# A fused attention and two-layer network kernel: the first 512 tokens by pairs of heads, parts of g and x out of PSUM, and rooms on the right 128 bytes further

## The chip, the cores and the metric

The kernel runs on one core of a Trainium2 chip. The metric is the device time of one execution in microseconds; the median of several runs is compared.

## The reference, cut to what matters

```python
def attention(q, k, v, g_norm):                  # [8 batches, 8 heads, 576, 64]
    kv = np.einsum('bhsd,bhse->bhde', k, v)      # one 64x64 matrix for each head
    out = np.einsum('bhsd,bhde->bhse', q, kv)
    rms = np.sqrt(np.mean(out * out, axis=-1, keepdims=True) + 1e-06)
    return out / rms * g_norm

x = attention(...).transpose(0, 2, 1, 3).reshape(4608, 512)   # tokens x heads*64
h = x @ w_in                       # 512 -> 2048
x = (h * np.cos(h)) @ w_out        # 2048 -> 512
h = x @ w_in2                      # 512 -> 1024
# softmax-weighted h, layer norm over 1024, then @ w_out2: 1024 -> 512
```

All inputs are float32, and some weights are rebuilt on the core from pairs of words.

## The kernel before, in words

Every large product is done as three float32r matmuls: high times high, high times low and low times high (`mm3`, lines 171 to 173). So each operand has to be split into a high part (a copy rounded to float32r) and a low part (operand minus high part).

The tokens are taken in nine blocks of 512 (`NB`, `TB`). The kernel has three stages. In the first (to about 305 us) attention is computed, and with it the *first quarter* of the first network: 4 of its 16 chunks of 128 hidden columns. A *step* is one block of tokens times one such chunk: `step_h` computes h = x @ w_in for it, in a PSUM bank, as 4 chunks of x (128 of the 512 features each) with 3 matmuls each; `cosine` makes g = h cos(h) and its two parts in six operations (a rounding on ScalarE, a subtraction on VectorE, a sine on ScalarE, the product on VectorE, the high part on ScalarE, the low part on VectorE); `step_out` multiplies g with w_out into four other banks. Steps alternate between banks 0 and 1. In the second stage (305 to 900 us) the other three quarters follow, by a scheme with seven products (`first_h`, `first_out`), in the third the second network (`second`, `soft`, `second_out`).

Attention goes by batches and tiles. `kv_slots` loads K and V of a batch's four pairs of heads, multiplies them (line 495), and copies the 64x64 results into the block-diagonal tile `kvf` (line 513). `tile_slots` takes a tile of 128 tokens: four q products into one bank (line 552), the square on ScalarE (560), the sum over each head on VectorE (562), a power on GpSimd (569 and 570), the norm on VectorE (584), four transposes back into the same bank (589), a scaled copy to `xf` on ScalarE (593), and for every second tile a store of `xf` to DRAM (597), which the second stage reads again. `pair_prep` then splits `xf` into the high and low part of x (lines 394 and 395). `convert` rebuilds a weight chunk (lines 366 to 377: a copy on ScalarE and five VectorE operations, the last of them on GpSimd for later weights), and `split` makes its parts.

All operations are handed to a planner (`Flow`), with a duration, a due time `at` and keys that they read and write. It works through them by its own durations: whenever an engine is free it takes the ready operation with the earliest `at`. That fixes the order on each engine's queue, SP's queue of DMAs included; on the chip each queue is worked off in that order, each instruction waiting for its inputs. `W_LOAD` holds the due times of the first eight weight loads. Operations on VectorE and GpSimd that both use SBUF exclude each other in the planner; those marked `ps=True` don't.

SBUF rooms are allocated from the left or from the right end. On the right lie `edge` (unused, 32 bytes a partition), then the attention pools, later `rxb`, `mid` and `rg2`. `rxa`, `rg`, `rwo` and the others lie on the left. The two attention banks after the first six uses are banks 6 and 7 in turn (`late_att`).

Of the kernel before, what the change touches and what calls it, by code (L numbers as in the profile page):

```python
# [17 lines left out]
P = 128  # L18
# [34 lines left out]
CV_AHEAD, W_LOAD = 15, (-40, -14, 0, 6, 10, 14, 18, 22)  # L53
# [106 lines left out]
def tile_kernel(ctx, tc, qkv, tail, g2, w1, w2, gl, out):  # L160
# [36 lines left out]
    declare("edge", "edge", 0, [P, 8])  # L197
# [154 lines left out]
    def convert(src, sk, yk, wk, at, load_at, on_dve, wide=1.3):  # L352
# [15 lines left out]
        add("DVE", 0.43, lambda: DVE.tensor_scalar(out=a(), in0=a(), scalar1=3, scalar2=None,  # L368
                                                   op0=ALU.logical_shift_left), r=[yk], w=[yk], at=at)
        add("DVE", 0.71, lambda: DVE.scalar_tensor_tensor(out=a(), in0=word(1), scalar=0x80000000, in1=a(),  # L370
                                                         op0=ALU.bitwise_and, op1=ALU.bitwise_or),
            r=[yk, sk, ("half", sk)], w=[yk], at=at)
        add("DVE", 0.43, lambda: DVE.tensor_scalar(out=buf[wk].bitcast(U32), in0=a(), scalar1=0xFF800000, scalar2=None,
# [107 lines left out]
    Q_CUTS = (0, 2 * P, S)  # L481

    def kv_slots(b):
        n, bks = ("kvf", b % 2), [att_bank() for _ in range(2)]

        def pair(bk, p, w, at):
            j = b * NPAIR + p
            kv, tl = kv_key("kv", j), kv_key("tl", j)

            def mm():  # L490
                for c in range(5):
                    for e in range(2):
                        k_, v_ = (buf[tl], P) if c == 4 else (buf[kv], 512)
                        at_ = e * D if c == 4 else c * P + e * D
                        PE.matmul(buf[bk][e * D:(e + 1) * D, p % 2 * D:(p % 2 + 1) * D], lhsT=k_[:, at_:at_ + D],  # L495
                                  rhs=k_[:, v_ + at_:v_ + at_ + D], start=(c == 0), stop=(c == 4))

            kv_load(j, at - (ATT_LEAD if b else 0))
            if b == 0:
                q_load(j, at + 3, Q_CUTS)  # L500
            add("PE", KV_T, mm, r=[kv, tl] + ([bk] if p % 2 else []), w=w + ([] if p % 2 else [bk]), at=at)

        def slot(half):
            def run(at):
                bk = bks[half]
                done = [("kvp", b, p) for p in range(2 * half, 2 * half + 2)]
                for i, d in enumerate(done):
                    pair(bk, 2 * half + i, [d], at)
# [24 lines left out]

    def tile_slots(g):
        bks = [att_bank() for _ in range(2)]

        def heads(ap):
            return ap.rearrange("p (n w) -> p n w", w=D)

        def first(h, at):  # L540
            t, i, bk, sq = 2 * g + h, (2 * g + h) % 4, bks[h], stage()
            for b, a, n, row in parts(t):
# [12 lines left out]
                for p in range(NPAIR):  # L555
                    add("PE", 0.222, lambda p=p, mm=mm: mm(p=p),
                        r=[kvf, *(("kvfh", kvf, i, e) for i in range(2) for e in range(2)), qs[p],
# [7 lines left out]
        def rms(h, at):  # L565
            i = (2 * g + h) % 4

            def power():
                POOL.tensor_scalar(out=buf["ss", i], in0=buf["ss", i], scalar1=1e-6, scalar2=None, op0=ALU.add)
                POOL.tensor_tensor(out=buf["y", i], in0=buf["ss", i], in1=buf["mhalf"], op=ALU.pow)  # L570

            add("POOL", POW, power, r=["mhalf"], w=[("ss", i), ("y", i)], at=at, ps=True)

        def second_(h, at):
# [18 lines left out]
            add("ACT", 0.61, lambda: ACT.activation(out=buf[xf][:, :, h * P:(h + 1) * P], in_=tr(), func=AF.Copy,  # L593
# [6 lines left out]
        def slot(h):  # L600
            def run(at):
# [3 lines left out]
                if h and g < NU - 2:  # L605
                    pair_prep(g, at - XPRI)
# [6 lines left out]
    def prep(src, keys, dst, hk, lk, at, lo_dve):  # L613
# [12 lines left out]
        def op(out_, fn, in0, in1, r, w):  # L626
            add("POOL", 0.75, lambda: POOL.tensor_tensor(out=out_(), in0=in0(), in1=in1(), op=fn), r=[*keys, *r], w=w, at=at)  # L627
# [15 lines left out]


# [3 lines left out]
    for i, name in enumerate(("xo0", "xo1", "rg2x")):  # L648
        for n in ("xhk", "xlk"):
            for j in range(4):  # L650
                flow.pool_of[n, i, j // 2, j % 2] = name

# [9 lines left out]
    def cosine(h, psrc, tk, n, hi, lo, r, hk, lk, t, on_dve):  # L662

        def tt():
# [9 lines left out]
        add("DVE", e_(0.71, 0.44, n), lambda: DVE.tensor_tensor(out=tt(), in0=h(), in1=tt(), op=ALU.mult),  # L674
            r=[*r, tk], w=[tk], at=t, ps=psrc)
# [538 lines left out]
```

## Time and profile before

| | us |
|---|---|
| median of 3 runs | 1290.01 (1287.57 to 1291.79) |
| profiled execution | 1292.3 |
| its span, first to last instruction | 1290.4 |
| TensorE busy | 1257.6 |
| VectorE / ScalarE / GpSimd busy | 930.3 / 677.9 / 518.3 |

The profile has a page of the whole execution and views of its trace: busy time by stage, groups of instructions by line, the waits and what released them, and the timeline. PE is TensorE, DVE is VectorE, ACT is ScalarE, POOL is GpSimd, SP the queue that issues the DMAs. Times are microseconds, or nanoseconds where it says so.

### The profile page before, as it was taken

How to read it: one execution, taken by the hardware profiler on the slowest of the kernel's cores; microseconds unless marked ns; L12 is line 12 of the kernel's file. 1: busy time of each engine (PE TensorE's matmuls, PEld its weight loads, DVE VectorE, ACT ScalarE, POOL GpSimd, SP SyncE). 2: the span in 40 equal slices, each digit the busy share in tenths (PEclk: the TensorE clock that was granted, in tenths of full speed). 3: DMA queues.
4: the chain of work that ended last, by engine and by line, in shares of the span. 5: the costliest groups of instructions: out<-in, count | busy, mean ns of one | idle time of the engine just before them, and what ended most of it. 6: DMA issues, size and time to landing. Idle time of an engine off the chain costs nothing.

```text
span 1290.4 us, 18723 instructions
## 1 busy us (share of the span) xinstructions
PE 1257.6 (97%) x6576; PEld 1066.5 (83%) x6576; DVE 930.3 (72%) x1544; ACT 677.9 (53%) x1225; POOL 518.3 (40%) x510
## 2 busy tenths in 40 slices
PE   5899999999999999999999999999999999999998
PEld 4688888887999899888788888887888888888887
DVE  6777777777887687878787766565777677776753
ACT  4666766675663563645364534442555545454533
POOL 2246656756745666554543443221321212121000
PEclk8899999999999999999999999999999999999999
DMA  8888899568948858663774374387111111111000
GB/s 278 292 264 283 286 326 304 191 216 282 336 152 227 285 184 276 211 227 115 241 221 157 101 212 136 107 284 237 59 56 50 50 42 56 43 50 42 25 25 33
DMA packets 177406, 224.59 MB, mean 174 GB/s; under 512 B 10912, under 2 KB 115360, under 8 KB 177312
## 3 DMA queue, kind: packets, MB, share of 16 engines
q1 hardware_dynamic: 177312, 223.39, 53.4%
q8 instruction: 52, 0.85, 0.3%
q14 instruction: 42, 0.34, 0.1%
HBM read 156.77 MB, written 66.58 MB: 173 GB/s over the span
## 4 chain that ended last, share of the span: by engine, by line
PE 75%; POOL 3%; DVE 3%; DMA 2%; issue 2%; ACT 1%; SPq 0%; POOLq 0%; ACTq 0%; DVEq 0%
PE ps L171 24%; PE ps L172 24%; PE ps L173 24%; PE ps L932 2%; POOL rg L677 1%; PE ps L552 1%; POOL fconv L419 1%; POOL fconv L377 1%; POOL ws L395 1%; DMA px<-fh 1%; PE ps L589 1%; DMA xf<-xd 0%; DMA bd<-ws 0%; PE ps L495 0%; DMA wid<-ws 0%
## 5 line engine op out<-in xcount | busy, mean ns | idle before, releaser
L171 PE MATMUL ps<-rg,rwo 128*128 128x512 f32 (+1 forms) x912 | 349.5, 383 | 1.6 <-ACT rg L676 1.6
L172 PE MATMUL ps<-rg,rwo 128*128 128x512 f32 (+1 forms) x912 | 346.6, 380 | 1.2 <-POOL rg L677 1.2
L173 PE MATMUL ps<-rg,rwo 128*128 128x512 f32 (+1 forms) x912 | 346.4, 380 | 0.0
L677 POOL TENSOR_TENSOR rg<-fh,rg 128x512 fp32r<-128x512 f32 (+1 forms) x120 | 149.3, 1253 | 174.4 <-ACT rg L676 161.5
L171 PEld LDWEIGHTS ps<-rg,rwo 128*128 128x128 f32 x912 | 171.9, 188 | 30.7 <-ACT rg L676 1.9
L172 PEld LDWEIGHTS ps<-rg,rwo 128*128 128x128 f32 x912 | 171.7, 188 | 30.3 <-POOL rg L677 2.2
L173 PEld LDWEIGHTS ps<-rg,rwo 128*128 128x128 f32 x912 | 171.6, 188 | 29.4
L914 POOL TENSOR_TENSOR const<-const,const 128x1 f32<-128x1 f32 x36 | 20.9, 580 | 333.2 <-DVE const L901 300.0
L171 PE MATMUL ps<-rxa,rwi 128*128 128x512 f32 (+1 forms) x384 | 147.3, 383 | 1.4 <-DVE fh L862 0.8
L172 PE MATMUL ps<-rxa,rwi 128*128 128x512 f32 (+1 forms) x384 | 145.6, 379 | 1.2 <-DVE rxa L395 1.2
L173 PE MATMUL ps<-rxa,rwi 128*128 128x512 f32 (+1 forms) x384 | 145.2, 378 | 0.0
L667 ACT ACTIVATE fh<-ps 128x512 int32<-128x512 f32 (+1 forms) x126 | 71.3, 567 | 103.4 <-PE ps L173 83.3
L672 ACT ACTIVATE fh<-fh,const 128x512 f32<-128x512 f32 (+1 forms) x156 | 106.6, 690 | 32.6 <-DVE fh L669 31.7
L171 PE MATMUL ps<-rxb,rwi 128*128 128x512 f32 (+1 forms) x288 | 112.7, 391 | 4.8 <-DVE fh L757 3.0
L676 ACT CAST rg<-fh 128x512 fp32r<-128x512 f32 (+1 forms) x156 | 90.6, 586 | 41.6 <-DVE fh L674 39.5
L173 PE MATMUL ps<-rxb,rwi 128*128 128x512 f32 (+1 forms) x288 | 110.4, 383 | 0.0
L172 PE MATMUL ps<-rxb,rwi 128*128 128x512 f32 (+1 forms) x288 | 109.9, 381 | 0.0
L669 DVE SCALAR_TENSOR_TENSOR fh<-ps,fh 128x512 f32<-128x512 f32 (+1 forms) x126 | 81.2, 648 | 28.3 <-ACT fh L667 25.6
L674 DVE TENSOR_TENSOR fh<-ps,fh 128x512 f32<-128x512 f32 (+1 forms) x126 | 80.9, 647 | 24.8 <-ACT fh L672 24.5
L627 POOL TENSOR_TENSOR sf<-xf 128x256 f32<-128x256 f32 x72 | 62.6, 876 | 61.9 <-DMA xf<-xd 32.5
L171 PEld LDWEIGHTS ps<-rxa,rwi 128*128 128x128 f32 x384 | 72.5, 189 | 14.5 <-DVE fh L862 1.3
L808 DVE TENSOR_TENSOR mid<-ps,mid 128x512 f32<-128x512 f32 (+1 forms) x90 | 56.9, 633 | 37.7 <-PE ps L173 37.2
(121 smaller groups left out, 2348.4 us busy)
## 6 DMA issues: line engine op xcount, KB each, us to landing
rwi<-wid SPq DMA_DIRECT2D x66, 512.0 KB, 5.7
rwo<-wod SPq DMA_DIRECT2D x88, 256.0 KB, 3.8
fconv<-w SPq DMA_DIRECT2D x36, 512.0 KB, 4.6
att<-qkv SPq DMA_DIRECT2D x32, 512.0 KB, 5.9
px<-fh SPq DMA_DIRECT2D x42, 256.0 KB, 4.2
xd<-xf SPq DMA_DIRECT2D x18, 512.0 KB, 3.9
wid<-ws SPq DMA_DIRECT2D x18, 512.0 KB, 4.7
xf<-xd SPq DMA_DIRECT2D x18, 512.0 KB, 5.2
```

What stands on the lines that cost most here:

```text
L171: PE.matmul(ps, lhsT=lh, rhs=rh, start=start, stop=False, skip_group_check=more)
L172: PE.matmul(ps, lhsT=lh, rhs=rl, start=False, stop=False, skip_group_check=more)
L173: PE.matmul(ps, lhsT=ll, rhs=rh, start=False, stop=stop, skip_group_check=more)
L627: add("POOL", 0.75, lambda: POOL.tensor_tensor(out=out_(), in0=in0(), in1=in1(), op=fn), r=[*keys, *r], w=w, at=at)
L667: add("ACT", e_(0.61, 0.42, n), lambda: ACT.activation(out=tt().bitcast(I32), in_=h(), func=AF.Copy, scale=INV_2PI, bias=0.25), r=r, w=[tk ...
L669: add("DVE", e_(0.71, 0.44, n), lambda: DVE.scalar_tensor_tensor(out=tt(), in0=h(), scalar=INV_2PI, in1=tt().bitcast(I32), op0=ALU.mult, o ...
L672: add("ACT", e_(0.74, 0.5, n), lambda: ACT.activation(out=tt(), in_=tt(), func=AF.Sin, bias=buf["halfpi"][:, 0:1], scale=TWO_PI), r=[tk, " ...
L674: add("DVE", e_(0.71, 0.44, n), lambda: DVE.tensor_tensor(out=tt(), in0=h(), in1=tt(), op=ALU.mult), r=[*r, tk], w=[tk], at=t, ps=psrc)
L676: add("ACT", e_(0.64, 0.42, n), lambda: ACT.copy(out=hi(), in_=tt()), r=[tk], w=hk, at=t + 2)
L677: either(on_dve, n, lambda eng: eng.tensor_tensor(out=lo(), in0=tt(), in1=f(hi()), op=ALU.subtract), [tk, *hk], lk, t + 2)
L808: add("DVE", e_(0.71, 0.44, n), lambda ak=ak, bk=bk: DVE.tensor_tensor(out=buf[ak][:, 0:n], in0=buf[bk][:, 0:n], in1=buf[ak][:, 0:n], op=A ...
L932: PE.transpose(tr()[:, c, :], buf["h2", n][:, (4 * q + c) * P:(4 * q + c + 1) * P], buf["ident"])
```

## The change

Four things are changed. First, the first 512 tokens of attention are no longer taken by tiles of 128 tokens and all heads, but by pairs of heads and all 512 tokens (`first_block`): each pair has its own bank, its own norm and transposes, and gives one chunk of x (128 features by 512 tokens). The matmuls of the first block's steps wait for one chunk (`xc`, `xcl`) instead of all of x. q's first cut is 512 tokens instead of 256, and the due times of three weight loads change. Second, for the later tiles the parts of x are made from PSUM right behind the transposes (`tile_prep`), instead of from `xf`; only the last two pairs of tiles keep `pair_prep`. Third, in `step_h` g stays in its PSUM bank, and both its parts are made from there (`there=True`); the low part is on VectorE as before. Fourth, `edge` grows from 32 to 160 bytes, and several durations that the planner reckons with change.

```diff
-CV_AHEAD, W_LOAD = 15, (-40, -14, 0, 6, 10, 14, 18, 22)
+CV_AHEAD, W_LOAD = 15, (-18.5, -12.5, -9, 6, 10, 14, 18, 22)
-    declare("edge", "edge", 0, [P, 8])
+    declare("edge", "edge", 0, [P, 40])
...
     def either(on_dve, n, fn, r, w, at):
         eng = DVE if on_dve else POOL
-        dur = e_(0.8, 0.44, n) if on_dve else e_(1.2, 0.7, n)
+        dur = e_(0.82, 0.5, n) if on_dve else e_(1.38, 0.8, n)
...
-    Q_CUTS = (0, 2 * P, S)
+    Q_CUTS = (0, TB, S)
...
+    def first_block(at, step):
+
+        kb = [att_bank() for _ in range(2)]
+        held[0], held[1] = xfs(), xfs()
+        kvf, scale = ("kvf", 0), buf["g2"][:, 0:1]
+        for p in range(NPAIR):
+            t = at + step * p
+            bk, sq, xn, q = att_bank(), stage(), xns(), ("q", p)
+            done = ("kvp", 0, p)
+            kv_pair(0, kb[p // 2], p, [done], t)
+            for e in range(2):
+                r, col = slice(e * D, (e + 1) * D), slice(p * P + e * D, p * P + (e + 1) * D)
+                add("ACT", 0.26, lambda r=r, col=col, p=p: ACT.copy(
+                    out=buf[kvf][r, col], in_=buf[kb[p // 2]][r, p % 2 * D:(p % 2 + 1) * D]),
...
+            def mm(p=p, bk=bk, q=q):
+                for i in range(TB // P):
+                    PE.matmul(buf[bk][:, i * P:(i + 1) * P], lhsT=buf[q][:, i * P:(i + 1) * P],
+                              rhs=buf[kvf][:, p * P:(p + 1) * P], start=True, stop=True)
+
+            add("PE", 0.45, mm, r=[kvf, ("kvfp", p, 0), ("kvfp", p, 1), q, ("qp", q, 0)], w=[bk], at=t)
+            add("ACT", 0.61, lambda sq=sq, bk=bk: ACT.activation(out=buf[sq], in_=buf[bk], func=AF.Square, scale=D ** -0.5),
+                r=[bk], w=[sq], at=t)
+            add("DVE", 0.68, lambda sq=sq, p=p: DVE.tensor_reduce(out=buf["ss", p], in_=heads(buf[sq]), axis=AX.X, op=ALU.add),
+                r=[sq], w=[("ss", p)], at=t)
+            power(p, t)
...
+            add("DVE", 0.71, norm, r=[bk, ("y", p)], w=[xn], at=t, ps=True)
+            add("PE", 0.45, turn, r=[xn, "ident"], w=[bk], at=t)
+            add("ACT", 0.66, lambda p=p, bk=bk: ACT.activation(out=xo(0, 0)[:, p, :], in_=buf[bk], func=AF.Copy, scale=scale),
+                r=[bk, "g2"], w=[("xc", p)], at=t)
+            add("DVE", 0.71, lambda p=p, bk=bk: DVE.scalar_tensor_tensor(
+                out=xo(0, 1)[:, p, :], in0=buf[bk], scalar=scale, in1=f(xo(0, 0)[:, p, :]), op0=ALU.mult, op1=ALU.subtract),
+                r=[bk, "g2", ("xc", p)], w=[("xcl", p)], at=t, ps=True)
+            for g in range(2):
+                xf = held[g]
+                add("ACT", 0.42, lambda g=g, xf=xf, p=p, bk=bk: ACT.activation(
+                    out=buf[xf][:, p, :], in_=buf[bk][:, g * 256:(g + 1) * 256], func=AF.Copy, scale=scale),
+                    r=[bk, "g2"] + ([xf] if p else []), w=[("xfp", g, p)] + ([] if p else [xf]), at=t + 10)
+        for g in range(2):
+            xf = held[g]
+            add("SP", 1.6, lambda g=g, xf=xf: SP.dma_start(out=xd[g], in_=buf[xf]),
+                r=[xf, *(("xfp", g, p) for p in range(NPAIR))], w=[("xd", g)], at=at + 30, lat=2.0)
...
             add("PE", 0.42, turn, r=[xn, "ident"], w=[bk], at=at)
+            if g < NU - 2:
+                tile_prep(g, h, tr, bk, at)
...
-                if h and g < NU - 2:
-                    pair_prep(g, at - XPRI)
...
+    def tile_prep(g, h, tr, bk, at):
...
+        add("ACT", 0.66, lambda: ACT.activation(out=xo(m, 0)[:, :, col], in_=tr(), func=AF.Copy, scale=scale),
+            r=[bk, "g2"], w=[hk], at=at)
+        add("DVE", 0.71, lambda: DVE.scalar_tensor_tensor(out=xo(m, 1)[:, :, col], in0=tr(), scalar=scale,
+                                                         in1=f(xo(m, 0)[:, :, col]), op0=ALU.mult, op1=ALU.subtract),
+            r=[bk, "g2", hk], w=[lk], at=at, ps=True)
...
+        g, gk = (h, r) if there else (tt, [tk])
+        add("DVE", e_(0.71, 0.44, n), lambda: DVE.tensor_tensor(out=g(), in0=h(), in1=tt(), op=ALU.mult),
+            r=[*r, tk], w=gk, at=t, ps=psrc)
+        add("ACT", e_(0.64, 0.42, n), lambda: ACT.copy(out=hi(), in_=g()), r=gk, w=hk, at=t + 2)
+        if there:
+            add("DVE", e_(0.71, 0.44, n), lambda: DVE.tensor_tensor(out=lo(), in0=g(), in1=f(hi()), op=ALU.subtract),
+                r=[*gk, *hk], w=lk, at=t + 2, ps=True)
+            return
...
         for k in range(KC):
-            add("PE", MM4, lambda k=k: mm(k), r=[*xk, ("w0", c), ("w0l", c)] + ([hb] if k else []), w=[hb], at=at)
+            x = xk if m else [*xk, ("xc", k), ("xcl", k)]
+            add("PE", MM4, lambda k=k: mm(k), r=[*x, ("w0", c), ("w0l", c)] + ([hb] if k else []), w=[hb], at=at)
...
+    first_block(-20, 3)
+    slots, needs = [], [0]
+    for g in range(2, NU):
...
-    run_slots(needs[0], -20, 1)
```

The planner's durations also change in `convert` (VectorE 0.43 to 0.55, 0.71 to 0.78, 0.43 to 0.48), in `prep` (GpSimd 0.75 to 0.9) and for the copy to `xf` (0.61 to 0.66).

## Rows read from the trace of the kernel before

**Rows 1.** Page, part 1: busy us, share, instructions of TensorE.
```profile
PE 1257.6 (97%) x6576; PEld 1066.5 (83%) x6576; DVE 930.3 (72%) x1544; ACT 677.9 (53%) x1225; POOL 518.3 (40%) x510
```
**Rows 2.** Windows by stage: length, busy by engine, granted clock, DMA share, GB/s.
```profile
core 0: us, PE busy (x) PEld busy (x) DVE busy (x) ACT busy (x) POOL busy (x), PEclk, DMA share, GB/s
0.00:64.00 64.00, 46.12 (x406) 37.42 (x407) 43.77 (x79) 33.66 (x61) 16.59 (x22) 0.87 0.84 284
64.00:305.00 241.00, 240.54 (x1570) 200.90 (x1569) 180.23 (x282) 161.13 (x299) 143.78 (x134) 1.00 0.82 268
305.00:640.00 335.00, 326.34 (x1655) 297.31 (x1653) 264.02 (x429) 174.55 (x331) 199.53 (x188) 0.99 0.70 227
640.00:900.00 260.00, 258.41 (x1111) 210.44 (x1112) 173.07 (x264) 117.69 (x198) 84.66 (x71) 0.99 0.60 188
```
**Rows 3.** Waits of TensorE, 0 to 64 us: total, times, longest.
```profile
PE ps L495 <- DMA att<-qkv: 8.2, 5, 6.1
PE ps L589 <- DVE att L584: 6.6, 3, 3.6
```
**Rows 4.** Timeline, 0 to 64 us: start, us, what, idle before and releaser.
```profile
6.08 1.34 PE L495 MATMUL ps<-att 128*64 128x64 f32 x20 [6.08 <-DMA att<-qkv]
...
11.89 1.34 PE L495 MATMUL ps<-att 128*64 128x64 f32 x20 [0.42 <-DMA att<-qkv]
...
13.16 4.86 PE L552 MATMUL ps<-att,att 128*128 128x128 f32 x32
...
15.27 0.60 ACT L560 ACTIVATE fh<-ps 128x512 f32<-128x512 f32 x1 [1.47 <-PE ps L552]
...
22.52 0.69 DVE L395 TENSOR_TENSOR rxa<-xf,rxa 128x512 fp32r<-128x512 f32 x1
...
29.18 0.69 DVE L395 TENSOR_TENSOR rxa<-xf,rxa 128x512 fp32r<-128x512 f32 x1
...
30.62 0.80 PE L171 MATMUL ps<-rxa,rg 128*128 128x512 f32 x1
...
35.30 0.39 PE L173 MATMUL ps<-rxa,rg 128*128 128x512 f32 x1
...
41.36 0.69 DVE L677 TENSOR_TENSOR rg<-fh,rg 128x512 fp32r<-128x512 f32 x1 [1.61 <-ACT rg L676]
...
42.23 0.48 PE L171 MATMUL ps<-rxa,rg 128*128 128x512 f32 x1
...
54.57 1.09 PE L589 MATMUL ps<-const,att 128*128 128x128 f32 x4 [3.60 <-DVE att L584]
...
61.67 0.68 DVE L395 TENSOR_TENSOR rg<-pa,rg 128x512 fp32r<-128x512 f32 x1
```
**Rows 5.** Windows of the start.
```profile
2.00:18.00 16.00, 10.12 (x112) 9.26 (x112) 6.68 (x14) 4.14 (x10) 1.24 (x2) 1.00 1.00 336
...
22.00:32.00 10.00, 7.16 (x55) 5.59 (x56) 8.53 (x15) 5.93 (x12) 3.26 (x3) 0.51 0.64 205
```
**Rows 6.** Timeline, one tile's bank, from the q products to the copy to xf.
```profile
101.65 1.06 PE L552 MATMUL ps<-att,att 128*128 128x128 f32 x8
...
109.55 0.69 ACT L593 ACTIVATE xf<-ps,const 128x512 f32<-128x512 f32 x1 [2.56 <-PE ps L589]
```
**Rows 7.** Timeline of SP's queue: the issue of two early weights.
```profile
31.97 1.21 SPq L364 DMA_DIRECT2D pa<-w  x2
```
**Rows 8.** DMA issues, 0 to 64 us: count, size, median us to landing.
```profile
pa<-w SPq DMA_DIRECT2D x4, 512.0 KB, 5.9
```
**Rows 9.** VectorE's groups by form, 64 to 305 us: busy, mean ns, idle before.
```profile
L395 DVE TENSOR_TENSOR rxa<-xf,rxa 128x512 fp32r<-128x512 f32 x24 | 20.6, 862 | 7.4 <-ACT rxa L394 7.4
```
**Rows 10.** Timeline of TensorE in the third stage: matmuls on rxa, then rxb.
```profile
986.91 0.39 PE L171 MATMUL ps<-rxa,rwi 128*128 128x512 f32 x1
...
988.95 0.40 PE L171 MATMUL ps<-rxb,rwi 128*128 128x512 f32 x1
...
990.34 0.39 PE L171 MATMUL ps<-rxa,rwi 128*128 128x512 f32 x1
```
**Rows 11.** Page, part 5: one of three lines of matmuls on rxb.
```profile
L171 PE MATMUL ps<-rxb,rwi 128*128 128x512 f32 (+1 forms) x288 | 112.7, 391 | 4.8 <-DVE fh L757 3.0
```

More of the change, by code (lines that the diff above doesn't have):

```diff
@@ L479, in q_load, with heads, kv_pair, mm @@
         flow.pool_of["qp", q, 0] = flow.pool_of["qp", q, 1] = flow.pool_of[q]
-    Q_CUTS = (0, 2 * P, S)
+    Q_CUTS = (0, TB, S)
+    def heads(ap):
+        return ap.rearrange("p (n w) -> p n w", w=D)
+    def kv_pair(b, bk, p, w, at):
+        j = b * NPAIR + p
+        kv, tl = kv_key("kv", j), kv_key("tl", j)
+        def mm():
+            for c in range(5):
+                for e in range(2):
+                    k_, v_ = (buf[tl], P) if c == 4 else (buf[kv], 512)
+                    at_ = e * D if c == 4 else c * P + e * D
+                    PE.matmul(buf[bk][e * D:(e + 1) * D, p % 2 * D:(p % 2 + 1) * D], lhsT=k_[:, at_:at_ + D],
+                              rhs=k_[:, v_ + at_:v_ + at_ + D], start=(c == 0), stop=(c == 4))
+        kv_load(j, at - (ATT_LEAD if b else 0))
+        if b == 0:
+            q_load(j, at + 3, Q_CUTS)
+        add("PE", KV_T, mm, r=[kv, tl] + ([bk] if p % 2 else []), w=w + ([] if p % 2 else [bk]), at=at)
     def kv_slots(b):
         n, bks = ("kvf", b % 2), [att_bank() for _ in range(2)]
[L486 to L501, printed above, removed]
         def slot(half):
@@ L507, in run @@
                 for i, d in enumerate(done):
-                    pair(bk, 2 * half + i, [d], at)
+                    kv_pair(b, bk, 2 * half + i, [d], at)
                 for e in range(2):
@@ L565, in rms @@
         def rms(h, at):
[L566 to L572, printed above, removed]
+            power((2 * g + h) % 4, at)
         def second_(h, at):
@@ L626, in op @@
         def op(out_, fn, in0, in1, r, w):
[L627 removed]
+            add("POOL", 0.9, lambda: POOL.tensor_tensor(out=out_(), in0=in0(), in1=in1(), op=fn), r=[*keys, *r], w=w, at=at)
         a = src
@@ L660, in pair_prep, with cosine @@
                   [("xhk", i, j, h)], [("xlk", i, j, h)], at, True)
-    def cosine(h, psrc, tk, n, hi, lo, r, hk, lk, t, on_dve):
+    def cosine(h, psrc, tk, n, hi, lo, r, hk, lk, t, on_dve, there=False):
         def tt():
@@ L965, in tile_kernel @@
     add("SP", 0.65, lambda: SP.dma_start(out=buf["gl"], in_=gl), w=["gl"], at=0, lat=1.0)
-    slots, needs = [], []
-    for g in range(NU):
-        b0 = parts(2 * g - 1)[-1][0] + 1 if g else 0
+    first_block(-20, 3)
+    slots, needs = [], [0]
+    for g in range(2, NU):
+        b0 = parts(2 * g - 1)[-1][0] + 1
         for b in range(b0, parts(2 * g + 1)[-1][0] + 1):
```

46 lines of the change are left out of this document (33 added, 13 removed).

## The prediction

> **What bounds the kernel now.** I read the busy shares first, then the same shares by stage, then what TensorE waited for at the start, then the timeline there. TensorE is busy 1257.6 of 1290.4 us [rows 1]: it is the bound, and only its 32.8 idle us, and its matmuls' own pace, can be given back. By stage [rows 2] it idles 17.9 us in the first 64, 0.5 in the 241 us from 64 to 305 (the rest of attention and the first quarter), 8.7 from 305 to 640 and 1.6 from 640 to 900. So what the change does to ScalarE, VectorE and GpSimd inside the first quarter can hardly gain; what it does to the first 64 us can.
>
> There TensorE waited 8.2 us for K and V and 6.6 us for normed tiles [rows 3]. In the timeline [rows 4] the reader is to see one long chain. The four K/V products run from 6.08 to 13.2, the four tiles' products end at 18.0, one tile then takes from 15.27 (square) to 23.21 (low part of x), and the last low part ends at 29.87, because the four tiles pass the same engines one after another. Only then, at 30.62, does the first step of the first quarter start, since its every matmul needs all four tiles. Its last matmul ends at 35.69, its cosine chain at 42.05, and the third step (the next in its bank) starts at 42.23. Much of this runs at the low clock: the granted clock is 0.51 from 22 to 32 us [rows 5], half of 2.4 GHz nearly throughout. A second stall, 3.6 us, ends at 54.57 [rows 3, 4], and the last early weight (chunk 3 of w_in) is split only at 62.35 [rows 4].
>
> **The change, part by part.**
>
> *Pairs of heads.* Sixteen logical q products, sixteen transposes, four squares, four reductions, four powers and four norms stay as many as they were; the tiles are cut by heads instead of tokens. TensorE's work is the same. New is that chunk k of x needs pair k alone, and the step's matmuls of chunk k wait for chunk k alone. So 9 of its 12 matmuls, and 9 of the second step's, can run before the last pair is there, in time in which TensorE idles today.
>
> When is the last pair there? The order on SP's queue changes: the first weight no longer leads, but two more stand ahead of the last q. In front of and with the first cut of q of pair 3 lie four K/V loads (512 KB), four tails (64), three weights (512), three whole q (288) and its own 256 KB: 4960 KB or 5.08 MB. The queue moved 336 GB/s from 2 to 18 us [rows 5], so 15.1 us from 2 on: 17.1. The same sum for what is loaded before the first K/V product now (1.11 MB) gives 5.3 where it started at 6.08, and for the fourth (2.88 MB) 10.6 where it started at 11.89 [rows 4]; I add 1.0: it lands at 18.1. From there: the products of one pair 1.2 (a quarter of the 4.86), the chain from square to low part 7.94 as the first tile shows it (15.27 to 23.21) [rows 4], less the 0.69 of the copy to xf [rows 6], which now comes behind the split: 7.25; 0.2 for the hand-over between them; and 1.0 for three VectorE operations that each find half of a 0.69 one in their way, as weights are converted in the same microseconds. Sum: 18.1 + 1.2 + 0.2 + 7.25 + 1.0 = 27.8. Three matmuls of step one are left, 0.80 for the first at the low clock [rows 4], say 1.5 together: step one ends at 29.3 instead of 35.7.
>
> *g and its parts in the bank.* The cosine chain has the same six operations, but its bank is free only behind the last, not behind the fourth. Now it takes 35.69 to 42.05, 6.4 us [rows 4]; so bank 0 is free at 35.7 and step three starts there, instead of at 42.23. The lead is 6.5 us. What fills TensorE from 29.3 to 35.7 is step two's rest and the second batch's K/V and tiles. Their loads now stand ahead of the stores of x on SP's queue.
>
> What moves with it. Weight 0 now comes behind the first K/V: with 1088 KB ahead and of its own it is in near 6.3; its eight operations of at most 0.69 end before 12, and the first chunk of x is there only at 16.7 (1.38 MB: 7.1, then the 9.65 as above). Weight 1, with 3.38 MB at 13.1, is split by 19, when chunk 1 is due. Both are hidden. The eight half copies to xf and the two stores of x go behind the last split, near 28.6; nobody reads these stores before the next stage, but SP's queue stands at them, and the weights behind them are late next. Today two of these are issued at 31.97 [rows 7] and take 5.9 to land [rows 8]: 38. In the new order the second batch and a weight (3968 KB), the stores (1024) and those two weights (1024) follow the 18.1: 6.16 MB at 336 GB/s, 18.3 us, so 36.4. That is a lead of only 1.6 us. But today's conversions drag on to 62.35 [rows 4] for want of VectorE, not of data, and that backlog starts 6.5 us earlier. **Start: -6.5.** Bounds: -2 if those loads decide, -12 if the 3.6 us stall and the slow matmuls after it (some 2 us) vanish too.
>
> *Parts of x from PSUM, later tiles.* Per tile the copy to the high part reads the bank instead of xf and the low part is a fused multiply-subtract out of the bank. VectorE's low part took 862 ns on average between 64 and 305 us, against 0.69 where GpSimd stood still [rows 9, 4]; out of PSUM it should be near 0.69. It saves VectorE 0.17 x 28 = 5 us, in a stage in which VectorE is busy 180 of 241 us and TensorE idles 0.5 [rows 2]. **0**, hidden by TensorE's own work; if that cover is gone it is worth at most those 5. The price is the bank, held 1.4 longer (rivals).
>
> *160 bytes on the right.* Rooms on the right (rxb, the attention pools) move by 128 bytes. The matmuls whose moving operand lies there have another pace than the others: six on rxb take 1.39 us from start to start, 232 ns each, nine on rxa just before 2.04 us, 227 ns [rows 10]. There are 3 x 288 on rxb [rows 11]: 864 x 5 ns = 4.3 us. No row shows such a room at another offset. Bounds: -4.3 (they take the common pace) and +4.3 (they lose as much again). A room moved off an odd place is likelier to have the common pace than a worse one; I take half: **-2**.
>
> *The planner's durations* (conversions, GpSimd operations, reductions). They alter no instruction, only the order on each queue. After 64 us that can touch the 8.7 idle us between 305 and 640 [rows 2]. Bounds: -4 (half of them go) and +4; I take **0**.
>
> Sum: -6.5 - 2 = -8.5. The profiled execution took 1292.3 us, 1290.4 of it span; the median of the runs is 1290.0. So I expect a span of about 1282 and a median of **1281.5 us**. Within 0.3% (3.9 us) a measurement can't tell a change from none: 1286.1 to 1293.9.
>
> **The rivals.**
>
> *The lead is kept (forecast)*: 1281.5, with 1277 to 1286 by the bounds of the rooms. Chance 0.52.
>
> *The lead is given back to weights*: TensorE gets steps one and two early and then waits for the two weights whose loads are only 1.6 us earlier. For it: those loads stay behind the stores. Against it: today they lie 4 to 5 us before they are converted. Time: 1290.0 - 2 for the start and, with the rooms at half of my value, - 1: 1287, within the bound. Chance 0.2; a part of it also stands for a change that in the end does nothing.
>
> *The second stall goes too*: with the stall at 54.57 and the slow stretch behind it gone, or the whole 4.3 of the rooms, 1290 - 12 - 2 = 1276. For it: VectorE's work is no more than before and starts earlier. Against it: its 44 us of work in the first 64 us [rows 2] must fit into some 52. Chance 0.2.
>
> *Slower: banks come free too late between 64 and 305.* A tile holds its bank from 101.65 to 110.24, 8.6 us [rows 6]; high and low part add 1.4. Two banks serve 28 tiles and 14 halves of K/V (about 3 us each, an estimate from the 1.34 for a pair's products [rows 4] and its copies): 14 x 10.0 + 7 x 3 = 161 of 241 us. It decides from a hold of (241 - 21)/14 = 15.7 us on; a hold of 17 would cost 14 x 1.3 = 18 us and give 1300. ScalarE's 161 busy us of 241 speak against such waits. The Trainium skill says (PSUM — Partial Sum Buffer, section PSUM bank collisions raise a hardware error) that two engines must not use one bank and the same partitions at once, reads against reads included, and that the compiler orders them. No row here shows two engines in one bank at a time; by that rule the copy to xf would wait for the low part, 0.7 us more, a hold of 10.7. Chance 0.08.
>
> Faster by over 0.3%: 0.52 + 0.2 + a little of the second, 0.74. Same: 0.18. Slower: 0.08. Range: from the full start and rooms, 1275, to the second rival with the rooms' upper bound in part, 1289.
>
> **What would show it.** Right: the first step's matmuls appear in threes from about 16 us on, the fourth three near 28, step three near 36, no 6 us wait at the start (first K/V product near 5); rxb matmuls at 227 ns. Wrong: the last q lands after 22 us; TensorE waits for a weight's low part between 40 and 55; idle from 305 to 640 well above 9 us; rxb at 232 ns or more (then 2 us are missing); L560 or L552 waiting for a bank between 64 and 305.

## The result, and the profile after

The changed kernel takes **1277.91 us** (median of 4 runs, 1274.10 to 1278.91), the kernel before 1290.42 beside it: a ratio of 0.9913 with a 95% interval of 0.9892 to 0.9934. The prediction was 1281.5, with a range of 1275 to 1289. Number and sign came out; the way there was another.

The profiled execution was the fastest of the four (1274.1 us, span 1272.3), and that of before (1292.3, span 1290.4) was slower than each of the four runs beside it (1287.57 to 1291.79), so the two traces lie 18.1 us apart where the medians lie 12.5.

The page of the changed kernel, TensorE's busy time and one of the three lines of matmuls on rxb:

```profile
PE 1241.3 (98%) x6576; PEld 1058.1 (83%) x6576; DVE 914.8 (72%) x1544; ACT 680.0 (53%) x1233; POOL 510.2 (40%) x510
...
L171 PE MATMUL ps<-rxb,rwi 128*128 128x512 f32 (+1 forms) x288 | 110.8, 385 | 0.4 <-DVE fh L751 0.4
```

Against [rows 1] TensorE is busy 16.3 us less with the same 6576 matmuls: what was won is mostly not idle time (part of it is the clock, below). The windows of the changed kernel, by stage and for the start:

```profile
0.00:64.00 64.00, 44.70 (x371) 34.29 (x371) 43.88 (x79) 34.19 (x67) 18.39 (x22) 0.97 0.80 266
64.00:305.00 241.00, 235.29 (x1581) 196.02 (x1581) 178.21 (x281) 162.03 (x300) 143.29 (x136) 1.00 0.83 273
305.00:640.00 335.00, 334.20 (x1721) 307.22 (x1720) 257.49 (x437) 179.30 (x343) 193.22 (x185) 1.00 0.72 231
640.00:900.00 260.00, 259.05 (x1151) 214.20 (x1150) 179.98 (x281) 121.20 (x205) 91.00 (x80) 1.00 0.58 184
22.00:32.00 10.00, 7.90 (x53) 5.06 (x52) 7.59 (x13) 6.08 (x13) 4.55 (x4) 1.00 0.90 296
```

Beside [rows 2] the first 64 us idle more (19.3 against 17.9), the next 241 us too (5.7 against 0.5), and the 335 after them hardly at all (0.8 against 8.7). Beside [rows 5] the stretch from 22 to 32 us runs at a granted clock of 1.00 (2.4 GHz) where it was 0.51, the lower of the two levels (1.2 GHz) nearly throughout. The second stage, counted from its first matmul on `rwi`, starts at 304.1 us instead of 299.2, behind the same 1944 matmuls: at that point the changed kernel is 4.9 us behind in these two traces, and all that it wins comes later.

The timeline of the changed kernel's start (start, us, what, idle before and releaser):

```profile
4.54 1.39 PE L495 MATMUL ps<-att 128*64 128x64 f32 x20 [4.54 <-DMA att<-qkv]
...
21.15 0.48 PE L171 MATMUL ps<-rxa,rg 128*128 128x512 f32 x1
...
23.52 0.58 SPq L364 DMA_DIRECT2D pa<-w  x1
...
32.81 0.40 PE L173 MATMUL ps<-rxa,rg 128*128 128x512 f32 x1
...
34.21 0.67 ACT L366 ACTIVATE pa<-pa 128x512 f32<-128x512 f32 x1
...
39.38 0.68 DVE L755 TENSOR_TENSOR rg<-ps,rg 128x512 fp32r<-128x512 f32 x1
...
41.34 0.69 DVE L395 TENSOR_TENSOR rg<-pa,rg 128x512 fp32r<-128x512 f32 x1
...
44.21 0.59 PE L171 MATMUL ps<-rxa,rg 128*128 128x512 f32 x1
```

The first step starts at 21.15 instead of 30.62, and its last matmul ends at 33.21. But the third step, which was to start near 36, starts at 44.21, where before it started at 42.23 [rows 4]. (In the two other profiles below whose queues have the same order up to there it starts at 43.96 and 42.65, so the 2 us between before and after are not clear of what differs from one execution to the next; that it does not come near 36 is.) Its bank is free at 40.06, behind the low part of the first step's g (L755). Its weight, chunk 2 of w_in, is issued at 23.52, is taken up by ScalarE only at 34.21, and its low part ends at 42.03. From 40.78 on TensorE works on q products that stand ahead of the step on its queue.

To see all kernels alike, each profiled span is split into TensorE's idle time, the busy time lost to the low clock, and the rest, which is the work at full clock. Idle time and clock come from windows of 4 us over the whole span; a window whose granted clock is under 0.985 counts its busy time times (1 - granted clock) as lost. "Time" is the median of the runs; the kernel before took 1290.4, 1287.8, 1287.9 and 1288.8 beside the changed kernel and the three sets of experiments.

| kernel | time | ratio to before (95%) | idle 0-64 | 64-300 | 300-900 | later | lost to clock | rest |
|---|---|---|---|---|---|---|---|---|
| before | 1290.4 | | 17.9 | 0.5 | 10.3 | 4.2 | 10.6 | 1246.9 |
| after | 1277.9 | 0.9913 (0.9892-0.9934) | 19.3 | 5.7 | 1.7 | 4.2 | 1.6 | 1239.7 |
| before + 160 bytes | 1282.0 | 0.9956 (0.9941-0.9970) | 17.4 | 1.0 | 10.6 | 4.2 | 7.0 | 1240.6 |
| before + durations | 1308.0 | 1.0155 (1.0139-1.0171) | 18.4 | 4.0 | 18.2 | 5.0 | 13.8 | 1246.8 |
| before + pairs | 1289.3 | 1.0011 (1.0000-1.0022) | 16.2 | 2.1 | 10.7 | 4.2 | 3.1 | 1251.0 |
| before + PSUM parts | 1282.3 | 0.9962 (0.9947-0.9976) | 20.8 | 2.2 | 2.1 | 4.2 | 5.7 | 1245.9 |
| after, 32 bytes | 1284.7 | 0.9969 (0.9955-0.9983) | 19.0 | 5.5 | 3.7 | 4.2 | 7.6 | 1245.9 |
| after, old durations | 1282.8 | 0.9960 (0.9941-0.9978) | 18.6 | 3.1 | 8.3 | 4.2 | 4.7 | 1238.6 |
| after, no PSUM parts | 1294.3 | 1.0043 (1.0027-1.0060) | 16.7 | 3.6 | 19.5 | 5.2 | 8.2 | 1240.4 |
| after, no pairs | 1288.4 | 1.0004 (0.9993-1.0016) | 18.9 | 7.0 | 9.0 | 4.2 | 9.4 | 1238.0 |
| before, light conversion | 1282.3 | 0.9955 (0.9940-0.9970) | 14.8 | 0.3 | 6.1 | 4.2 | 5.4 | 1246.8 |
| before + pairs, light | 1282.9 | 0.9959 (0.9946-0.9973) | 14.6 | 1.4 | 9.8 | 4.2 | 3.0 | 1251.2 |
| after, low part first | 1271.0 | 0.9870 (0.9854-0.9886) | 18.0 | 3.8 | 2.6 | 4.2 | 1.3 | 1239.1 |
| after, one duration 0.92 | 1277.2 | 0.9910 (0.9891-0.9929) | 17.9 | 5.7 | 4.8 | 4.2 | 4.4 | 1239.4 |

Between the two traces -7.2 us are work at full clock, -9.0 the clock and -1.9 idle time (+1.4, +5.2, -8.5 and 0 by stage). The share of the clock is partly that of the two executions chosen: the runs of before beside the first set of experiments had mean clocks of 0.991 to 0.996, its profiled one 0.989; those of after 0.993 to 0.999.

### The profile page after: what moved, and what is told of

It is laid out like the page before. It is cut to its first block, busy times and chain, and to the rows that moved or that the text cites. A ratio compares the mean times of both kernels' runs of the same rounds, so it can differ in the third digit from the quotient of the medians.

```text
span 1272.3 us, 18770 instructions
## 1 busy us (share of the span) xinstructions
PE 1241.3 (98%) x6576; PEld 1058.1 (83%) x6576; DVE 914.8 (72%) x1544; ACT 680.0 (53%) x1233; POOL 510.2 (40%) x510
## 4 chain that ended last, share of the span: by engine, by line
PE 88%; DVE 3%; POOL 3%; DMA 2%; ACT 2%; issue 1%; SPq 0%; ACTq 0%; POOLq 0%; DVEq 0%
PE ps L171 27%; PE ps L173 27%; PE ps L172 27%; PE ps L1014 2%; PE ps L613 2%; POOL att L540 1%; PE ps L495 1%; DMA wid<-ws 1%; DMA px<-fh 1%; PE ps L645 1%; DMA att<-qkv 1%; POOL att L539 0%; POOL fconv L377 0%; POOL ws L395 0%; ACT xf L651 0%
## 5 line engine op out<-in xcount | busy, mean ns | idle before, releaser
L758 POOL TENSOR_TENSOR rg<-fh,rg 128x512 fp32r<-128x512 f32 (+1 forms) x120 | 146.0, 1230 | 141.9 <-ACT rg L753 124.7
L171 PE MATMUL ps<-rxb,rwi 128*128 128x512 f32 (+1 forms) x288 | 110.8, 385 | 0.4 <-DVE fh L751 0.4
L172 PE MATMUL ps<-rxb,rwi 128*128 128x512 f32 (+1 forms) x288 | 108.4, 376 | 0.0
L173 PE MATMUL ps<-rxb,rwi 128*128 128x512 f32 (+1 forms) x288 | 108.3, 376 | 0.0
L744 DVE SCALAR_TENSOR_TENSOR fh<-ps,fh 128x512 f32<-128x512 f32 (+1 forms) x126 | 81.5, 648 | 29.6 <-ACT fh L742 27.8
L395 POOL TENSOR_TENSOR ws<-fconv,ws 128x512 fp32r<-128x512 f32 (+1 forms) x52 | 65.9, 1271 | 44.8 <-ACT ws L394 40.2
L377 POOL TENSOR_TENSOR fconv<-fconv 128x512 f32<-128x512 f32 x40 | 53.3, 1333 | 73.8 <-DVE fconv L375 68.4
```

The source lines that it names most:

```text
L171: PE.matmul(ps, lhsT=lh, rhs=rh, start=start, stop=False, skip_group_check=more)
L172: PE.matmul(ps, lhsT=lh, rhs=rl, start=False, stop=False, skip_group_check=more)
L173: PE.matmul(ps, lhsT=ll, rhs=rh, start=False, stop=stop, skip_group_check=more)
L377: either(on_dve, 512, lambda eng: eng.tensor_tensor(out=buf[wk], in0=buf[yk], in1=buf[wk], op=ALU.add), r=[yk, wk], w=[wk], at=at)
L395: either(on_dve, n, lambda eng: eng.tensor_tensor(out=lo(), in0=src(), in1=f(hi()), op=ALU.subtract), [*keys, *hk], lk, at)
L744: add("DVE", e_(0.71, 0.44, n), lambda: DVE.scalar_tensor_tensor(out=tt(), in0=h(), scalar=INV_2PI, in1=tt().bitcast(I32), op0=ALU.mult, o ...
```

## Experiments: each part alone

The theory to be tested was the prediction's sum (start -6.5, rooms -2, the rest 0); the rival, that the parts work through the order on the queues, and so do not add.

**160 bytes alone.**

```diff
-    declare("edge", "edge", 0, [P, 8])
+    declare("edge", "edge", 0, [P, 40])
```

> The kernel before with the 160 bytes alone. Theory of the rooms: TensorE's matmuls get a faster pace wherever rooms on the right are in use, so from 305 to 900 us all of them (on rg too) go from 228 to 232 ns to about 227, 2700 matmuls by some 3 ns: 7 to 8 us faster, near 1283; the waits of TensorE stay. Rival, the pace belongs to the execution and not to the room: 1290 within 2 us, pace as before.

1282.0 us, ratio 0.9956: -5.7 us. Effects are given here and below as the difference of ratios times 1288 us, since the sets of runs lie apart by 2.6 us. Every queue has the order of before, and the waits are nearly the same (idle 17.4, 1.0, 10.6). From start to start a matmul on rxb (512 columns) went from 232 to 227 ns. And there were others: the groups of matmuls by form from 305 to 900 us, first of the kernel before, then of this one (the last figures are busy us, mean ns of one, idle before):

```profile
L172 PE MATMUL ps<-rg,rwo 128*128 128x512 f32 x292 | 114.4, 392 | 0.2 <-POOL rg L677 0.2
```
```profile
L172 PE MATMUL ps<-rg,rwo 128*128 128x512 f32 x297 | 115.7, 389 | 0.3 <-POOL rg L677 0.3
```

The matmuls on rg gain 3 ns each in the mean (230 to 227 from start to start). Four of rg's twelve rooms in the second stage are `rg2` and lie on the right too, and in the trace of before the matmuls on rg come in two kinds, groups of three at 226 to 227 ns and groups at 224 to 238; with 160 bytes nearly all are at 226 to 227. Paired one by one between the two traces, the matmuls on rxb gained 3.3 us in all and those on rg 3.4 in the second stage. The theory's pace came out; its 7 to 8 us were 5.7. The rooms are one common effect: in the table the rest is 1245.9 to 1246.9 with 32 bytes and 1238.0 to 1240.6 with 160 (the two kernels with pairs alone, 1251.0 and 1251.2, stand apart; see below).

**The planner's durations alone** (six lines, nine numbers, named with the diff; no operation changed).

```diff
-        dur = e_(0.8, 0.44, n) if on_dve else e_(1.2, 0.7, n)
+        dur = e_(0.82, 0.5, n) if on_dve else e_(1.38, 0.8, n)
...
-            add("POOL", 0.75, lambda: POOL.tensor_tensor(out=out_(), in0=in0(), in1=in1(), op=fn), r=[*keys, *r], w=w, at=at)
+            add("POOL", 0.9, lambda: POOL.tensor_tensor(out=out_(), in0=in0(), in1=in1(), op=fn), r=[*keys, *r], w=w, at=at)
```

> The kernel before with the planner's new durations alone. Theory of the order: the 10 us of waits between 305 and 900 us and the two drops of the clock behind them (some 5 us) go, 8 to 14 us faster, 1276 to 1282; the matmuls' pace stays at 228 to 232 ns. Rival, the order of the queues has no part in the gain: 1290 within 3 us, with as much idle time between 305 and 900.

1308.0: 20.0 us slower, so neither the theory's gain nor the rival's nothing. The two longest waits of TensorE between 299 and 900 us in this kernel:

```profile
PE ps L171 <- ACT rxa L394: 8.4, 1, 8.4
PE ps L171 <- ACT rxb L394: 4.9, 1, 4.9
```

And what stood on GpSimd's queue ahead of the first of them, then the matmul that waited:

```profile
313.01 0.74 POOL L627 TENSOR_TENSOR sf<-xf 128x256 f32<-128x256 f32 x1
313.70 3.10 POOL L419 TENSOR_TENSOR fconv<-fconv 128x256 f32<-128x256 f32 x4
319.59 2.48 POOL L395 TENSOR_TENSOR ws<-fconv,ws 128x512 fp32r<-128x512 f32 x2 [2.79 <-ACT ws L394]
322.03 0.72 POOL L627 TENSOR_TENSOR sf<-sf,xf 128x256 f32<-128x256 f32 x1
...
323.46 0.69 PE L171 MATMUL ps<-rxa,rwi 128*128 128x384 f32 x1 [8.40 <-ACT rxa L394]
```

L627 makes the sums of x (`sf`) that the second stage's first block needs. A weight job's four operations (L419) and two more stand between two of them, with a 2.79 us wait of their own: 8.3 us from 313.75 to 322.03, which is nearly the 8.4 that TensorE stands still. The last of these sums ends 35 us after the second stage has begun (302.5), in the changed kernel 17 us after (304.1). The granted clock falls in and behind this wait, as it does at the two other long ones: in the table 13.8 us go to the low clock.

**Pairs of heads alone** (`first_block` with its loads, without the three other parts).

```diff
+    first_block(-20, 3)
...
-    run_slots(needs[0], -20, 1)
```

> The kernel before with the first 512 tokens by pairs of heads, the new due times of the weight loads and the waits by chunk, alone. Prediction: the lead of 6.5 us is kept, near 1283.5, and the second stage starts near 292.5 instead of 299.2. Rival, the lead is given back before 305 us: step 4 begins about 3 us earlier than at 65.5, but the second stage starts at 297 to 301, 1290 within 4 us.

1289.3: +1.4 us, no gain. The windows of this kernel:

```profile
0.00:64.00 64.00, 47.81 (x419) 37.98 (x419) 44.60 (x81) 35.14 (x69) 17.08 (x22) 0.95 0.82 277
64.00:305.00 241.00, 238.91 (x1557) 199.28 (x1557) 178.61 (x278) 160.40 (x298) 143.71 (x134) 1.00 0.82 269
...
22.00:32.00 10.00, 8.15 (x54) 5.88 (x56) 7.17 (x12) 5.04 (x11) 1.91 (x2) 0.83 0.76 259
```

The first step came at 19.8 instead of 30.6, but the third at 43.4, and the second stage began at 299.2, to a tenth as before. Against the trace of before, idle time in the first 64 us fell by 1.7 us and the clock's loss by 7.5 (2.9 of it in the first 64 us); against them stand 4.1 us more work at full clock and 1.6 idle between 64 and 300. Why the work at full clock grows here, and again in the other kernel with pairs but without the rest, stays open.

**Parts of g and x from PSUM alone** (`tile_prep`, and g left in its bank).

```diff
+            if g < NU - 2:
+                tile_prep(g, h, tr, bk, at)
...
-                if h and g < NU - 2:
-                    pair_prep(g, at - XPRI)
...
-                [hb], [("gs", j)], [("gsl", j)], at, True)
+                [hb], [("gs", j)], [("gsl", j)], at, True, True)
```

> The kernel before with the parts of g and of x from PSUM alone. Prediction: 0, hidden under TensorE's work, 1290 within 3 us and TensorE idle under 1 us from 64 to 305. Rival, banks and the queues that wait for them come late: 4 to 6 us of idle time from 64 to 305 as in the changed kernel, 1294 to 1296.

1282.3: -4.9 us, neither 0 nor the rival's loss. It idles more in the first 300 us (23.0 against 18.4), but loses the second stage's waits. Its window from 305 to 640 us:

```profile
305.00:640.00 335.00, 333.70 (x1706) 305.59 (x1705) 269.83 (x445) 179.43 (x342) 197.15 (x185) 1.00 0.73 237
```

1.3 us idle against 8.7 [rows 2]. The tiles are done by then: the last low part of x from PSUM in the changed kernel starts at 237.9.

## Experiments: the change less one part

> The changed kernel with the rooms back at 32 bytes. Theory of the rooms: it loses what the 160 bytes gave alone (ratio 0.9956, 5.7 us, 8 us of it in the second stage): 1283 to 1285, matmuls on rxb back at 232 ns, those on rg at 230 in the second stage, idle time as in the changed kernel. Rival, the rooms help only together with another order: 1278 within 2.

The 160 bytes undone (the first diff above, reversed): 1284.7, ratio 0.9969: 7.2 us more than the changed kernel (0.9913). The matmuls are back at 230 ns on rg and 232 on rxb, from 227 on both. Every queue has the order of the changed kernel. Yet this profile lost 5.9 us to the low clock in its first 64 us, where the changed kernel's lost 1.6: so much can lie between two executions of one order.

> The changed kernel with the planner's old durations. Alone the new ones cost 20 us, by 18 us of waits after 300 us. Theory: durations change nothing but the order of the queues, and what an order costs in waits after 300 us is not a sum of the parts: the result lies anywhere from 1272 to 1300, and follows the idle time between the start of the second and of the third stage (1.8 us in the changed kernel) one to one, with the clock's drops on top. Rival, the durations cost 20 us here too, so without them 1258.

The old durations in the changed kernel: 1282.8, ratio 0.9960: 6.1 us more. So the same numbers that cost the kernel before 20 us bring this one 6; its waits sit between 300 and 900 us again (8.3).

> The changed kernel with the parts of g and x made from SBUF as before. If what these parts gave alone (4.9 us) came from a better order of the queues after 300 us, the second stage has other waits than 1.8 us and the time goes with them; if it came from VectorE and the banks in the first stage, the second stage starts later than at 304 us. By the trace of these parts alone (298.2 against 299.2 us) I expect the first.

The parts made from SBUF again: 1294.3, ratio 1.0043: 16.7 us more, slower than the kernel before. The two longest waits of TensorE between 299 and 900 us, and GpSimd's queue ahead of the longest:

```profile
PE ps L171 <- ACT rxa L394: 8.9, 1, 8.9
PE ps L171 <- DMA rwo<-wod: 5.2, 1, 5.2
```
```profile
305.79 0.74 POOL L683 TENSOR_TENSOR sf<-xf 128x256 f32<-128x256 f32 x1
306.49 3.10 POOL L419 TENSOR_TENSOR fconv<-fconv 128x256 f32<-128x256 f32 x4
...
315.42 0.72 POOL L683 TENSOR_TENSOR sf<-sf,xf 128x256 f32<-128x256 f32 x1
```

The same picture as with the durations alone: the four L419 stand between the first block's sums, and 8.9 us after the end of the sum ahead of them the next one starts. In the kernels before, after and with pairs alone the four come behind the first block's sums, with PSUM parts alone behind all but the last, and no such wait is there. With the old durations they stand between the sums too, but two by two, and the longest wait is 2.3 us. That moving them alone would take the wait away was not tried.

> The changed kernel without the pairs of heads (first 512 tokens by tiles, old due times of the weight loads). Alone the pairs gave nothing (ratio 1.0011), since the third step still starts at 43.4 us. Theory: nothing here either, but for the waits after 300 us: 1278 plus the difference of these waits. Prediction's view: it loses 6.5 us, 1284 to 1285, and the second stage starts 6 us later than at 304.

The tiles of before in the changed kernel: 1288.4, ratio 1.0004: 11.7 us more. Idle time is 39.1 us against 31.0, 7.3 of the difference after 300 us, and 9.4 us are lost to the low clock against 1.6. The second stage starts at 309.8, 5.7 us later than in the changed kernel and behind the same 1944 matmuls, as the prediction's view had it (6 us), but not by its mechanism: up to 300 us the idle time differs by only 0.9 us, the clock's loss by 6.3. The third step starts at 43.6, as with the pairs.

So the four parts alone give -5.7, +20.0, +1.4 and -4.9, together +10.8; taking each one out costs 7.2, 6.1, 16.7 and 11.7, together 41.7; all four give -11.2 (0.9913). Only the rooms are worth about the same in both, and the sum of parts is no account of this change.

## Experiments: the third step, the bank, the order

**What holds the third step?** The suspicion was VectorE's work for weights. In two kernels the eight early weights are converted by one VectorE operation per half instead of five: the kernel before, as a control, and the kernel with pairs alone.

```diff
+        if on_dve:
+            add("DVE", 0.71, lambda: DVE.tensor_tensor(out=buf[wk], in0=buf[yk], in1=buf[yk], op=ALU.add),
+                r=[yk, sk, ("half", sk)], w=[wk], at=at)
+            return
```

> The kernel before, with the eight early weights' conversion cut to one ScalarE and one VectorE operation per half (four of the five VectorE operations left out, so the early weights' values are not the reference's). It is the control for the next kernel. Theory (VectorE's conversions hold the third step): the third step's matmul comes earlier than 42.2 us, near 40, or stays at 42 because the cosine's chain alone gives that; second stage starts 1 to 3 us before 299.2. Rival (the conversions have cover): third step at 42 to 43, second stage at 299. Time 1284 to 1292 by either, since the waits of the second stage move with every order (2 to 20 us of idle so far).

> The kernel before with the pairs of heads alone, and the same light conversion as the control (the early weights' values are not the reference's). Theory: in the kernel with pairs alone the first step came 10.8 us earlier but the third at 43.4, because the third's w_in chunk waited for its conversion behind the pairs' own VectorE work; with four of five VectorE operations gone the third step comes at 36 to 38 us, TensorE's idle time in 0 to 64 falls by 4 to 7 us against the control, and the second stage starts 4 to 7 us before the control's. Rival (the third step is held by something else, for instance the chain of the last pair or a DMA): third step still at 42 to 44 and second stage within 1.5 us of the control's.

The theory fell. The control's third step came at 41.6 us, that with pairs at 42.8; both idle alike in the first 64 us (14.8 and 14.6), and the times are 1282.3 and 1282.9. The lighter conversion alone is worth 6 us (it leaves work out), the pairs nothing beside it. The weight of the third step in the kernel with pairs and light conversion, from its load's issue to its first matmul:

```profile
22.90 0.58 SPq L364 DMA_DIRECT2D pa<-w  x1
...
37.26 0.68 ACT L366 ACTIVATE pa<-pa 128x512 f32<-128x512 f32 x1
...
39.79 0.68 DVE L399 TENSOR_TENSOR rg<-pa,rg 128x512 fp32r<-128x512 f32 x1
...
42.81 0.40 PE L171 MATMUL ps<-rxa,rg 128*128 128x512 f32 x1
```

In the control the same copy stood at 34.15 and waited for its data:

```profile
34.15 0.67 ACT L366 ACTIVATE pa<-pa 128x512 f32<-128x512 f32 x1 [0.98 <-DMA pa<-w]
```

With the pairs the load is issued 6.2 us earlier than the control's 29.09, and it lands at 28.8. But ScalarE takes it up at 37.26, without a wait for it: its queue has the first step's cosine ahead of it. The low part ends at 40.47, and TensorE has matmuls of w_out and K/V ahead of the third step until 42.81. So what held the step in this trace is the place on the queues, first ScalarE's, then TensorE's. What it would bring to put that copy ahead of the cosine was not tried.

**Two engines on one bank.** In the changed kernel ScalarE's copy to xf and VectorE's low part of x both read the tile's bank and nothing that the other writes, but they go one after the other. VectorE's group in the changed kernel, 64 to 305 us:

```profile
L724 DVE SCALAR_TENSOR_TENSOR rxa<-ps,const,rxa 128x512 fp32r<-128x512 f32 x24 | 18.0, 751 | 13.3 <-ACT xf L651 8.9 <-PE ps L495 2.2 <-ACT rxa L722 1.8
```

That is 8.9 us, in 15 waits: VectorE, whose low part the next steps need, waits for a copy that they don't need. So the order was turned: the copies read the low part's key.

```diff
-                    r=[bk, "g2"] + ([xf] if p else []), w=[("xfp", g, p)] + ([] if p else [xf]), at=t + 10)
+                    r=[bk, "g2", ("xcl", p)] + ([xf] if p else []), w=[("xfp", g, p)] + ([] if p else [xf]), at=t + 10)
...
-                r=[bk, "g2"] + ([xf] if h else []), w=[(xf, h)] + ([] if h else [xf]), at=at)
+                r=[bk, "g2", *([("xlk", xkey(g // 2), g % 2, h)] if g < NU - 2 else [])] + ([xf] if h else []), w=[(xf, h)] + ([] if h else [xf]), at=at)
```

> The changed kernel, with ScalarE's two copies to xf made after VectorE's low part of x out of the same bank, where the changed kernel issues the copy first and the low part waited 8.9 us in all (15 times) for it. Theory (two engines on one bank go one after the other, and the order decides who waits): the low part's wait on the copy goes to under 2 us, the copy waits in its place, TensorE's idle time in 64 to 304 falls from 5.7 to 1 to 3 us and the second stage starts at 300 to 302. Rival: the 5.7 us are something else (weights), and stay at 4 to 7. The time: 1273 to 1278 if the second stage's waits stay near 1.8 us, up to 1290 if the new order brings such waits as the single parts had.

1271.0 us, the fastest of all: 0.9870 (0.9854 to 0.9886) of the kernel before, where the changed kernel has 0.9913. The wait is gone:

```profile
L724 DVE SCALAR_TENSOR_TENSOR rxa<-ps,const,rxa 128x512 fp32r<-128x512 f32 x24 | 17.9, 748 | 5.5 <-ACT rxa L722 5.3
```

TensorE idles 3.8 us between 64 and 300 instead of 5.7 (1 to 3 were expected), and 1.3 less in the first 64. The second stage starts at 294.7, earlier than expected, and lasts 6.1 us longer, so work went over the border with it. TensorE's order differs from the start of the kernel on; what of the 5.5 us by which the two ratios differ is the wait and what the order, these runs don't separate.

**A tiny change of the order.** One duration of GpSimd 0.92 in place of 0.90, which changes TensorE's order from its 1963rd matmul on, at 307.9 us; on the other queues the first difference comes at 277.8.

```diff
-            add("POOL", 0.9, lambda: POOL.tensor_tensor(out=out_(), in0=in0(), in1=in1(), op=fn), r=[*keys, *r], w=w, at=at)
+            add("POOL", 0.92, lambda: POOL.tensor_tensor(out=out_(), in0=in0(), in1=in1(), op=fn), r=[*keys, *r], w=w, at=at)
```

> The changed kernel with one of the planner's durations for GpSimd 0.92 in place of 0.90: no operation is added, removed or resized; TensorE's order of instructions is the same up to about its thousandth and differs in places behind it. Theory (the order of the queues behind 300 us, not the parts' work, makes the differences of 5 to 20 us between these kernels): the second stage's idle time leaves 1.8 us, to anything from 1 to 20 us, the pace of matmuls stays at 226.5 to 227.5 ns, the second stage starts at 304.1, and the time differs from the changed kernel's by 2 us or more. Rival (a planned duration must be far off to matter): idle 1.5 to 3 us and the time within 2 us of 1277.9.

1277.2, ratio 0.9910, that of the changed kernel. Idle time from 300 to 900 us did move, from 1.7 to 4.8. The 4.4 instead of 1.6 us that went to the low clock lie in the first 90 us, where every queue has the changed kernel's order, so they belong to the execution. The ratios agree. Neither side had it whole: this other order brought 3 us of waits and no time that the runs can show.

## Why the number came out, step by step

**Pairs of heads, -6.5: the step that failed.** The prediction had the last q at 18.1, the last low part of x at 27.8 and the end of the first step at 29.3. The q landed at 19.5, but its products started only at 22.80, behind a copy of K/V that stood on ScalarE's queue behind copies to xf; the low part ended at 32.42 and the step at 33.21, 3.9 us late. The miss that mattered was "bank 0 is free at 35.7 and step three starts there". The bank was free at 40.06, and even then the step had to wait: the conversion of chunk 2 of w_in ended at 42.03, and TensorE had q products to finish until 44.21. The prediction followed weights 0 and 1 and the two issued at 31.97 [rows 7], but not this one, issued at 28.90 before and done at 39.75, just under the cover of the bank's 42.05. With the cover gone it was next. That is the second rival's mechanism (the lead is given back to a weight), though by the engines' queues and not by the load. What stayed in the first 64 us of the two traces is the clock: 1.6 us lost instead of 6.0, with 1.4 more idle, so -3.0 in place of -6.5. Even this is not all shown to be the pairs' doing: the profiles of the six kernels with tiles lost 5.4 to 6.7 us there and seven of the eight with pairs 0 to 3.1, but the eighth, the changed kernel with 32 bytes, lost 5.9. By the start of the second stage nothing of it was left (304.1 against 299.2).

**Parts from PSUM, 0.** Right for the first quarter, where they cost idle time rather than gained it. Wrong for the second stage, which the argument never asked about: 8 us of waits are away there with these parts alone, and since the tiles are done by then, the order that the planner makes is what is left to explain it. The bank cost far less than the fourth rival's price. TensorE's waits in the changed kernel that bear on it, the first from 0 to 64 us, the others from 64 to 305:

```profile
PE ps L613 <- DVE rxa L724: 2.1, 2, 1.7
```
```profile
PE ps L645 <- DVE att L640: 2.7, 3, 1.4
PE ps L171 <- DVE rg L755: 1.4, 2, 1.1
PE ps L495 <- DVE rxa L724: 0.3, 1, 0.3
```

L613 and L495 write the bank next and wait for the low part out of it: 0.3 us between 64 and 305. Most of the 5.7 us of idle time there waited for normed tiles (L640), for the low part of g (L755) and once for a ScalarE operation (1.3). Without these parts 3.6 of the 5.7 us are still there, and alone they add 1.7. The rule that the prediction quoted from the Trainium skill (PSUM — Partial Sum Buffer, section PSUM bank collisions raise a hardware error), that two engines must not use one bank and the same partitions at once and are put in order, agrees with the trace: L724 waited for L651, which only reads. But the wait fell on the low part, not on the copy.

**160 bytes, -2: right in kind, too small.** rxb took the common pace of 227 ns, and rg2, which the prediction left out, lies on the right as well: the work at full clock went from 1246.9 to 1240.6, so -6.3 in the trace and -5.7 in time.

**The durations, 0 within 4.** The bound was wrong in kind: it let a new order only take away or add about half of the 8.7 idle us that were there. A new order can set up waits that were not there, 8.4 us for one, and the clock fell behind the long ones: +20 alone, -6 with the other parts.

**The sum.** -8.5 predicted, -12.5 measured by the medians. By the two traces, which lie 18.1 us apart, the start brought 3.5 us less than predicted within its 64 us; by the runs with 160 bytes alone the rooms brought 3.7 more; 5.2 us of idle time between 64 and 300 and -13.1 from 300 to 900 (8.5 idle, 4.6 clock) had no term at all. The near agreement is partly luck.

## What to carry to other kernels

When a planner orders the queues, a changed duration is a change of the kernel: look at the order around each stage's first consumer, and expect neither that parts add nor that a stretch without edits stays as it was. When a wait is taken away, list everything that ended just under its cover, weights that are converted on other engines above all, and look where each stands on its queue and not only when its data lands. Where two engines read one bank, try letting the one go first whose result is waited for (here that took 8.9 us of VectorE's waits away; how much of the 5.5 us came from it isn't separated).

## What the hardware showed that was not expected

A matmul's pace depended on where its moving operand lies: on rxb 232 ns with rooms behind 32 bytes and 227 behind 160, 128 bytes further on, with every queue in the same order, and 232 again when the 160 were taken back in the changed kernel. Other offsets were not measured, and why the place matters stays open.

In these rows TensorE's clock fell behind its waits, and the loss came on top of the wait. In the kernel before, the matmul that ended its longest second-stage wait, and the window around it:

```profile
640.77 0.79 PE L171 MATMUL ps<-rxb,rwi 128*128 128x512 f32 x1 [3.01 <-DVE fh L757]
```
```profile
640.00:648.00 8.00, 7.23 (x19) 5.72 (x20) 5.14 (x10) 4.65 (x8) 2.56 (x3) 0.58 1.03 360
```

3.0 us of waiting, and a mean granted clock of 0.58 over 8 us, near the lower level (1.2 GHz), in which 7.23 busy us lost 3.0 more (7.23 x 0.42). The changed kernel, without such a wait, held 1.00 in the same window. So did the kernel with 160 bytes alone, behind a wait of 2.0 us that ended at 639.2: the clock did not fall behind every wait.
